# A four-byte GpSimd copy ahead of GpSimd's last five additions, in an attention and mixture-of-experts kernel

## The chip, the cores and the metric

The kernel runs on one core of a Trainium2 chip. The metric is the device time of one execution in microseconds (us); lower is better. Times given are medians of several runs. The engines are TensorE (matrix products, PE in the profile; its weight loads are PEld), VectorE (DVE), ScalarE (ACT), GpSimd (POOL) and SyncE (SP), which here only issues transfers. Each engine runs its own instructions in order and waits on semaphores for the others.

## What is computed

The reference is linear attention with an exponential feature map, and then a layer of eight experts whose outputs are mixed by a normalised routing table `P`:

```python
proj = x @ w_phi; proj -= max(abs(proj))
phi(x) = concat(exp(proj), exp(-proj))
num = phi(q) @ (phi(k).T @ v);  den = phi(q) @ phi(k).sum() + 1e-6
x = num / den                          # 4608 x 512
...
for e in range(8):
    h = maximum(x @ w1[e], 0)          # 512 -> 1024
    out += P[:, e:e+1] * (h @ w2[e])   # 1024 -> 512
```

The change concerns the last two additions into `out`, for expert 7 and the last rows.

## The kernel before

The 4608 rows are nine groups of 512. Attention comes first, together with expert 0; then experts 1 to 7 each go over the groups. For every group the products with `w1` and `w2` are done by a Strassen scheme of seven products on quarters, with sums and differences of quarters made beforehand.

`down7(e, g, H, B7, last)` makes the second product of group `g` and expert `e`. Its left operands are the quarters of the hidden layer `H` and four sums of them, `S[0]` to `S[3]`, made by VectorE as eight instructions of 128x512 (line 1013, in the helper `sub`): each of the four in two halves `h`. `S[3]`, half 1, is the last of the eight. For the very last call, group 7 of expert 7 (`last`), these four stand in buffers of the ring `hT`, so the profile calls them hT; for other groups they are called S.

The seven products, eight matmuls each, are called X1, Y1, Z1, X2, X3, Z2, X4. They go into three PSUM banks: X1, X2, X3 and X4 accumulate in one bank, Z1 and Z2 in another. After each product its bank is read out, scaled by the column of `P`, and added to a quarter of the accumulator `acc[g]`; the next product into the same bank has to wait for that read. There are two ways to read. VectorE does it in one instruction per 128x256 (line 1306). Or ScalarE copies the scaled bank into a buffer `U` or `V` (line 1316, two instructions) and GpSimd adds the 128x512 buffer to `acc` (line 1320).

The last two groups of expert 7 are 6 and 7; they are called a and b here. Their fourteen products are asked for in the order `END` (line 1390). In group 6 only aX1 goes by way of GpSimd; in group 7 bX1, bY1, bZ1 and bX3 do. These are GpSimd's last five additions. aX1 and aY1 add to the same quarter of `acc[6]`, so VectorE's accumulation for aY1 waits for GpSimd's addition for aX1. Stores of finished quarters (line 982) are issued by SP; nine of them belong to these two groups.

What sets the order of instructions is the class `Plan`. Each operation is recorded with the engine it runs on, an estimated duration, and keys that it reads and writes. `schedule` lays the operations out in time by these, and the program is then written in that order. Keys are only names for the planner: the semaphore waits of the program come from the memory that instructions read and write. `"sums of h"` is such a key. It is written by the last difference of each group, and the five last additions read it (line 1323). So the planner places them behind the last difference of group 7, but nothing in the memory that they touch makes them wait for it on the chip.

Of the kernel before, what the change touches and what calls it, by code (L numbers as in the profile page):

```python
# [9 lines left out]
FP32 = mybir.dt.float32  # L10
# [218 lines left out]
def kernel(  # L229
# [11 lines left out]
    nc = tc.nc  # L241

    B, H, S, D = q.shape
# [57 lines left out]
    def pool(el, fn, r=(), w=()):  # L301
        plan.op("POOL", el * 1.64e-3 + 0.17, 0.25, fn, r, w, shared=True)
# [56 lines left out]
    def new(tag):  # L359
        return banks.new(int(tag[1])) if tag in ("P1", "P2") else R[tag].new()  # L360
# [472 lines left out]
    for i, (queue, eng) in enumerate((("ACT", nc.scalar), ("POOL", nc.gpsimd))):  # L833
        dma(queue, 1 << 15, 100, lambda i=i, eng=eng: eng.dma_start(
            out=wphi_f[64 * i:64 * i + 64, :], in_=w_phi), w=[f"wphi_f{i}"])
# [4 lines left out]
    for i in range(2):  # L840
        dve(64, lambda i=i: nc.vector.tensor_copy(
            out=wphi2[64 * i:64 * i + 64, i, :], in_=wphi_f[64 * i:64 * i + 64, :]),
# [4 lines left out]
    for h0 in (4, 6):  # L847
# [3 lines left out]
        out=wgate, in_=moe_w_gate.rearrange("(c p) e -> p c e", p=128)), w=["wgate"])  # L851
# [157 lines left out]
    def sub(eng, el, out_, x, y, op, r, w):  # L1009
        f = nc.vector if eng is dve else nc.gpsimd  # L1010
        kw = {"shared": True} if eng is dve else {}
        eng(el * 0.6 if eng is dve else el * 1.04 + 128,
            lambda: f.tensor_tensor(out=out_(), in0=x(), in1=y(), op=op), r, w, **kw)  # L1013
# [228 lines left out]
    def down7(e, g, H, B7, last=False):  # L1242


        def part(i, j, h):
            return lambda: H[j][h]()[:, :, 256 * i:256 * i + 256]

        def hk(i, j, h=None):
            if h is None:
                return hk(i, j, 0) + hk(i, j, 1)  # L1250
            return [(H[j][h], i)] if g == 8 else [(H[j][h], n) for n in range(2)]
# [5 lines left out]
        S = [new("hT" if last else "S") for _ in range(4)]  # L1257

        def sv(n):
            return S[n]().rearrange("p a b -> p (a b)").rearrange("p (a b) -> p a b", a=4)  # L1260

        def sh(n, h):
            return lambda: sv(n)[:, 2 * h:2 * h + 2, :]
# [22 lines left out]
        for h in range(2):  # L1286
            sub(dve, 512, sh(3, h), part(0, 1, h), sh(1, h), ALU.subtract,
                [(S[1], h)] + hk(0, 1, h), [(S[3], h)] + (["sums of h"] if h else []))

        def prod(bank, lhs, y, r, first, more=()):  # L1290
            f, r2 = B7[y]
            product(bank, lhs, lambda k: f()[:, k, :], 4,
                    r + r2 + (["P"] if e else late) + list(more), first)
# [32 lines left out]
        if e == 1 and g < 9:  # L1326
            for ts in range(4):
                act(512, lambda ts=ts: nc.scalar.activation(
                    out=acc[g][:, ts, :], in_=acc[g][:, ts, :], func=ACT.Copy, bias=0.0,
# [64 lines left out]
    def pop():  # L1394
        if not queue:
            return None
        e, g, H, B7 = queue.pop(0)
        return down7(e, g, H, B7, (e, g) == (E - 1, 7))

    for e in range(1, E):  # L1400
        w1, w2 = load_w(e, ["late"] + [("acc", 8, ts, j) for ts in range(4) for j in range(2)
                                       if e > 1])
        if e == 1:
# [3 lines left out]
            for p in range(4):  # L1407
                seen = {}
# [52 lines left out]
```

## Time and profile before

| | |
|---|---|
| median of 3 runs | 1035.03 us (1034.81 to 1035.73) |
| the profiled execution, its own time | 1034.76 us |
| its span in the profile | 1032.9 us |
| TensorE busy | 1007.7 us (98% of the span) |
| VectorE busy | 874.4 us (85%) |
| ScalarE busy | 707.5 us (68%) |
| GpSimd busy | 466.8 us (45%) |
| mean granted TensorE clock | 0.997 |

The profile comes from one execution. All times in it count from the start of its span. A matmul's end is modelled, and successive matmuls overlap in the record, so their pace is read from one start to the next. The timeline merges instructions of one kind that follow each other: start, length from the first start to the last end, what, and how many. Brackets hold the idle time before, and who ended it. The granted clock is the share of its full speed that TensorE's clock had.

### The profile page before, as it was taken

The page shows a single profiled execution, that of the slowest core. Times are in us where ns is not written, and L with a number is a line of the kernel's source. Part 1 is how long each engine was busy: PE and PEld are TensorE (multiplying, and loading weights), DVE is VectorE, ACT ScalarE, POOL GpSimd, SP SyncE. Part 2 cuts the span into 40 slices and gives each one's busy share as a digit, 9 for nine tenths or more (in the row PEclk, how much of TensorE's full clock was granted, in tenths as well). Part 3 has the DMA queues.
Part 4 walks back from the last instruction along what each step waited for, and adds up shares of the span by engine and source line. Part 5 has one row for each costly group of instructions (what it writes and reads, how often), then busy time and mean ns, then how long its engine had stood idle before and what let it go on. Part 6 is the DMA issues. An engine that isn't in the chain of part 4 may idle for free.

```text
span 1032.9 us, 21788 instructions
## 1 busy us (share of the span) xinstructions
PE 1007.7 (98%) x7856; PEld 692.4 (67%) x7974; DVE 874.4 (85%) x1875; ACT 707.5 (68%) x1571; POOL 466.8 (45%) x535
## 2 busy tenths in 40 slices
PE   7899999999999999999999999999999999999997
PEld 5666666644566766676667666676667666776665
DVE  7999998987787888888878888888888888887887
ACT  7999999845688766566666665666666665656662
POOL 5877775400244444434444354435343444344443
PEclk9999999999999999999999999999999999999998
DMA  9998985095311152122511161106111421104323
GB/s 259 179 171 143 183 156 103 2 230 145 75 43 51 52 107 58 42 63 51 114 42 54 40 128 48 41 22 123 48 47 52 99 65 42 62 22 123 133 92 123
DMA packets 124700, 93.77 MB, mean 91 GB/s; under 512 B 47456, under 2 KB 116640, under 8 KB 124592
## 3 DMA queue, kind: packets, MB, share of 16 engines
q1 hardware_dynamic: 90832, 68.44, 24.3%
q0 software_dynamic: 33680, 23.90, 16.2%
q8 instruction: 62, 1.02, 0.4%
q14 instruction: 46, 0.38, 0.1%
q10 hardware_dynamic: 80, 0.03, 0.0%
HBM read 94.98 MB, written 14.16 MB: 106 GB/s over the span
## 4 chain that ended last, share of the span: by engine, by line
PE 90%; DVE 6%; DMA 1%; issue 1%; ACT 1%; SPq 0%; POOL 0%; DVEq 0%; ACTq 0%
PE P L1130 40%; PE P L1164 30%; PE P L484 17%; DVE acc L1306 1%; PE P L683 1%; DMA acc<-in_q_dram 1%; DVE hT L1194 1%; DVE m L476 1%; DVE w L1013 1%; PE P L722 1%; DVE hT L1013 1%; DVE S L1013 0%; SPq L406 0%; PE P L688 0%; DVE xb L703 0%
## 5 line engine op out<-in xcount | busy, mean ns | idle before, releaser
L1320 POOL TENSOR_TENSOR acc<-acc,V 128x512 f32<-128x512 f32 x244 | 313.9, 1298 | 433.4 <-ACT V L1316 430.0
L1190 ACT COPY U<-P 128x512 f32<-128x512 f32 x378 | 216.2, 588 | 133.4 <-PE P L1164 68.9
L1316 ACT ACTIVATE V<-P 128x256 f32<-128x256 f32 x488 | 212.8, 477 | 122.1 <-PE P L1130 118.6
L1194 DVE CUSTOM_DVE_ANT_0 hT<-P,U 128x512 bf16<-128x512 f32 x378 | 252.3, 687 | 36.6 <-ACT U L1190 21.0
L1130 PEld LDWEIGHTS <-S 128*128 128x128 bf16 x1984 | 194.5, 98 | 56.0 <-issue 3.0
L1306 DVE SCALAR_TENSOR_TENSOR acc<-P,acc 128x256 f32<-128x256 f32 x384 | 164.7, 478 | 72.4 <-PE P L1130 69.9
L1164 PE MATMUL P<-xT,w 128*128 128x512 bf16 x682 | 193.3, 379 | 1.8 <-DVE acc L1306 0.6
L1130 PEld LDWEIGHTS <-hT 128*128 128x128 bf16 x1544 | 151.4, 98 | 56.4 <-DVE hT L1194 0.7
L1164 PE MATMUL P<-xT,T 128*128 128x512 bf16 x544 | 156.8, 379 | 1.6
L1130 PE MATMUL P<-w,hT 128*128 128x256 bf16 x1016 | 146.7, 273 | 0.4 <-DVE hT L1194 0.3
L1130 PE MATMUL P<-T,S 128*128 128x256 bf16 x1056 | 137.7, 273 | 2.8 <-DVE acc L1306 2.6
L1164 PEld LDWEIGHTS <-w 128*128 128x128 bf16 x896 | 87.6, 98 | 61.2 <-issue 0.7
L1130 PE MATMUL P<-w,S 128*128 128x256 bf16 x928 | 124.1, 273 | 1.1
L1013 DVE TENSOR_TENSOR S<-hT 128x512 bf16<-128x512 bf16 x248 | 105.1, 439 | 19.3 <-PE P L1130 18.3
L1164 PEld LDWEIGHTS <-T 128*128 128x128 bf16 x672 | 65.7, 98 | 58.0 <-issue 1.8
L476 DVE TENSOR_REDUCE m<-P 128x4 f32<-128x512 f32 x128 | 83.7, 679 | 3.4 <-PE P L484 2.4
L609 POOL TENSOR_TENSOR v<-v_m,em 128x512 bf16<-128x512 f32 x64 | 66.9, 1045 | 43.2 <-ACT em L480 39.1
L1199 ACT ACTIVATE hT<-P 128x512 bf16<-128x512 f32 x126 | 74.2, 598 | 11.7 <-PE P L1164 11.4
L484 PE MATMUL P<-xT,w 128*128 128x512 bf16 x271 | 71.7, 379 | 0.9 <-ACT q L480 0.3
L1130 PE MATMUL P<-T,hT 128*128 128x256 bf16 x528 | 71.3, 275 | 0.0
L484 PE MATMUL P<-w,hT 128*128 128x512 bf16 x272 | 69.7, 379 | 0.8 <-DVE m L476 0.2
L480 ACT ACTIVATE k<-P 128x512 bf16<-128x512 f32 x128 | 68.8, 633 | 2.2 <-PE P L484 1.3
(109 smaller groups left out, 1178.5 us busy)
## 6 DMA issues: line engine op xcount, KB each, us to landing
xT<-xd SPq DMA_DIRECT2D x168, 128.0 KB, 2.2
w<-in_moe_w_dram POOLq DMA_DIRECT2D x14, 1024.0 KB, 9.9
v_m<-in_v_dram SPq DMA_DIRECT2D x14, 512.0 KB, 5.1
out_dram<-acc SPq DMA_DIRECT2D x12, 512.0 KB, 3.1
X<-xd SPq DMA_DIRECT2D x42, 128.0 KB, 2.2
early<-xd SPq DMA_DIRECT2D x42, 128.0 KB, 2.2
xd<-S SPq DMA_DIRECT2D x18, 256.0 KB, 2.9
qk<-in_k_dram POOLq DMA_DIRECT2D x12, 256.0 KB, 5.5
```

Of the source, the lines that this page charges most:

```text
L476: dve(el, lambda: nc.vector.tensor_reduce(out=dst(), in_=src(), axis=AX.X, op=ALU.max, apply_absolute_value=True), r, w)
L480: act(el, lambda: nc.scalar.activation(out=dst(), in_=src(), func=ACT.Exp, bias=0.0, scale=scale), r, w)
L484: nc.tensor.matmul(out_, lhsT=lhsT, rhs=rhs, start=start, stop=stop)
L1013: lambda: f.tensor_tensor(out=out_(), in0=x(), in1=y(), op=op), r, w, **kw)
L1130: pe(256, lambda i=i, k=k, z=z: nc.tensor.matmul(bank()[:, 256 * i:256 * i + 256], lhsT=lhs(k, i), rhs=rhs(k), start=first and z, stop=k = ...
L1164: pe(512, lambda k=k: nc.tensor.matmul(bank[fp](), lhsT=f()[:, k, 128 * fp:128 * fp + 128], rhs=rhs(k), start=first and k == 0, stop=k == ...
L1190: act(512, lambda: nc.scalar.copy(out=u[fp][n]().rearrange("p a b -> p (a b)"), in_=x[fp]()), [x[fp]], [u[fp][n]])
L1194: dve(500, lambda: nc.vector._custom_dve(ADD_SAT, out=out_(fp, i, j), in0=halves_(bank[fp]()), in1=flat(u[fp][n]()), s0=3.0e38, s1=0.0), [ ...
L1199: act(512, lambda: nc.scalar.activation(out=out_(fp, i, j), in_=halves_(x[fp]()), func=ACT.Relu, bias=0.0, scale=1.0), [x[fp]], [okey(fp, ...
L1306: dve(330, lambda n=n, ts=ts: nc.vector.scalar_tensor_tensor(out=acc[g][:, ts, 256 * j:256 * j + 256], in0=bank()[:, 256 * n:256 * n + 256 ...
L1316: act(390, lambda n=n: nc.scalar.activation(out=u()[:, n, :], in_=bank()[:, 256 * n:256 * n + 256], func=ACT.Copy, bias=0.0, scale=P[:, 4 ...
L1320: pool(670, lambda: nc.gpsimd.tensor_tensor(out=acc[g][:, 2 * i:2 * i + 2, 256 * j:256 * j + 256], in0=acc[g][:, 2 * i:2 * i + 2, 256 * j: ...
```

## The change

When `down7` is called for group 7 of expert 7, one GpSimd copy is recorded behind the differences. It copies one 32-bit word per partition, the last two bf16 columns of `S[3]`, half 1, into a fresh buffer that nothing reads. For the planner it also writes `"sums of h"`.

```diff
         for h in range(2):
             sub(dve, 512, sh(3, h), part(0, 1, h), sh(1, h), ALU.subtract,
                 [(S[1], h)] + hk(0, 1, h), [(S[3], h)] + (["sums of h"] if h else []))
+        if last:
+            seen = new("rr")
+            pool(4, lambda: nc.gpsimd.tensor_copy(
+                out=seen()[:, 0:1], in_=sv(3)[:, 3, 254:256].bitcast(FP32)),
+                [(S[3], 1)], [seen, "sums of h"])
```

The order of TensorE, VectorE and ScalarE stays as it was. On two engines something moves. First GpSimd's end, from the last addition of group 5 on. Rows show the line, the operation, what it writes and reads, its size, and the semaphores that it waits for, which are named after the engine that raises them. acc6_4271 and acc7_4272 are the accumulators of groups 6 and 7. Before:

```order
L1320 TENSOR_TENSOR acc5_4270<-acc5_4270,V_13995 128x2x256 [waits Activation_49]
L1320 TENSOR_TENSOR acc6_4271<-acc6_4271,U_14057 128x2x256 [waits Activation_49]
L1320 TENSOR_TENSOR acc7_4272<-acc7_4272,U_14068 128x2x256 [waits Activation_49]
L1320 TENSOR_TENSOR acc7_4272<-acc7_4272,U_14097 128x2x256 [waits Activation_49,Pool_49]
L1320 TENSOR_TENSOR acc7_4272<-acc7_4272,U_14112 128x2x256 [waits Activation_49]
L1320 TENSOR_TENSOR acc7_4272<-acc7_4272,U_14162 128x2x256 [waits Activation_49,Pool_49]
```

These are the additions for aX1, bY1, bX1, bZ1 and bX3. The same place in the changed program, where line 1320 has become line 1325, and L1291 is the copy:

```order
L1325 TENSOR_TENSOR acc5_4270<-acc5_4270,V_13995 128x2x256 [waits Activation_49]
L1291 COPY rr_14090<-hT_14077 128x1 [waits DVE_49]
L1325 TENSOR_TENSOR acc6_4271<-acc6_4271,U_14057 128x2x256 [waits Activation_49]
L1325 TENSOR_TENSOR acc7_4272<-acc7_4272,U_14068 128x2x256 [waits Activation_49]
L1325 TENSOR_TENSOR acc7_4272<-acc7_4272,U_14114 128x2x256 [waits Activation_49]
L1325 TENSOR_TENSOR acc7_4272<-acc7_4272,U_14099 128x2x256 [waits Pool_49]
L1325 TENSOR_TENSOR acc7_4272<-acc7_4272,U_14163 128x2x256 [waits Activation_49,Pool_49]
```

The copy, with its wait for VectorE, stands ahead of all five additions, and the additions for bZ1 and bX1 have changed places (third and fourth). Second, SP's stores of the two groups; the first six of the nine, before:

```order
L982 DMA out_0_dram<-acc6_4271 128x2x256 [waits DMAHW3_49,DVE_49,Pool_49]
L982 DMA out_0_dram<-acc7_4272 128x2x256 [waits DMAHW4_49,Pool_49]
L982 DMA out_0_dram<-acc6_4271 128x2x256 [waits DMAHW5_49,DVE_49]
L982 DMA out_0_dram<-acc6_4271 128x2x256 [waits DMAHW6_49,DVE_49]
L982 DMA out_0_dram<-acc7_4272 128x2x256 [waits DMAHW7_49,DVE_49]
L982 DMA out_0_dram<-acc6_4271 128x256 [waits DMAHW0_49,DVE_49]
```

and in the changed program:

```order
L982 DMA out_0_dram<-acc6_4271 128x2x256 [waits DMAHW3_49,DVE_49,Pool_49]
L982 DMA out_0_dram<-acc6_4271 128x2x256 [waits DMAHW4_49,DVE_49]
L982 DMA out_0_dram<-acc7_4272 128x2x256 [waits DMAHW5_49,Pool_49]
L982 DMA out_0_dram<-acc6_4271 128x2x256 [waits DMAHW6_49,DVE_49]
L982 DMA out_0_dram<-acc7_4272 128x2x256 [waits DMAHW7_49,DVE_49]
L982 DMA out_0_dram<-acc6_4271 128x256 [waits DMAHW0_49,DVE_49]
```

The store of group 7's first quarter, which waits for GpSimd, has gone from second to third place.

## The prediction

> **What bounds it.** I read the page first, then the chain of waits, then the last 24 us engine by engine. TensorE is busy for 98% of the span and heads the chain nearly throughout, so a change to GpSimd's last five additions can matter only where TensorE stops. The page and the chain (start, length, what) say where:
>
> ```profile
> span 1032.9 us, 21788 instructions
> PEclk9999999999999999999999999999999999999998
> ...
> 1013.25 5.89 DVE hT L1013 x8
> 1019.98 6.21 PE P L1130 x40
> ```
>
> The chain leaves TensorE at 1010 us for VectorE; its largest piece there is the eight differences of the last group (L1013, into hT buffers). The granted clock is full in all slices but the last. TensorE's timeline for the end (start, length from first start to last end, tile, count; in brackets the idle time and its releaser):
>
> ```profile
> 1016.37 1.04 PE L1130 MATMUL P<-T,hT 128*128 128x256 bf16 x8
> 1019.98 1.10 PE L1130 MATMUL P<-T,S 128*128 128x256 bf16 x6 [2.57 <-DVE acc L1306]
> 1020.87 1.92 PE L1130 MATMUL P<-T,hT 128*128 128x256 bf16 x8
> 1022.57 0.63 PE L1130 MATMUL P<-T,S 128*128 128x256 bf16 x2
> 1023.00 1.42 PE L1130 MATMUL P<-w,S 128*128 128x256 bf16 x8
> 1024.26 0.49 PE L1130 MATMUL P<-w,hT 128*128 128x256 bf16 x3
> 1024.59 1.04 PE L1130 MATMUL P<-T,hT 128*128 128x256 bf16 x8
> 1025.46 0.71 PE L1130 MATMUL P<-w,hT 128*128 128x256 bf16 x5
> 1026.01 1.91 PE L1130 MATMUL P<-T,hT 128*128 128x256 bf16 x16
> ```
>
> With a and b for groups 6 and 7, the rows are bZ1, aX3 (six), bX2, aX3 (two), aZ2, bZ2 (three), bX3, bZ2 (five), aX4 with bX4. At full clock eight matmuls take 0.87 us (1024.59 to 1025.46), 0.109 each. bZ1 would hand over at 1016.37 + 0.87 = 1017.24; aX3 starts at 1019.98, 2.74 us late, because VectorE had not yet read aX2 out of the bank that aX3 accumulates into. VectorE's and GpSimd's timelines say why:
>
> ```profile
> 1013.16 5.98 DVE L1013 TENSOR_TENSOR hT<-hT 128x512 bf16<-128x512 bf16 x8
> 1014.50 0.42 DVE L1013 TENSOR_TENSOR hT<-hT 128x512 bf16<-128x512 bf16 x1
> 1014.84 1.49 DVE L1013 TENSOR_TENSOR hT<-hT 128x512 bf16<-128x512 bf16 x1
> 1016.25 1.48 DVE L1013 TENSOR_TENSOR hT<-hT 128x512 bf16<-128x512 bf16 x1
> 1017.66 1.48 DVE L1013 TENSOR_TENSOR hT<-hT 128x512 bf16<-128x512 bf16 x1
> 1019.06 2.43 DVE L1306 SCALAR_TENSOR_TENSOR acc<-P,acc 128x256 f32<-128x256 f32 x6
> 1019.46 0.47 DVE L1306 SCALAR_TENSOR_TENSOR acc<-P,acc 128x256 f32<-128x256 f32 x1
> 1022.82 2.52 DVE L1306 SCALAR_TENSOR_TENSOR acc<-P,acc 128x256 f32<-128x256 f32 x6 [1.33 <-PE P L1130]
> 1026.21 2.62 DVE L1306 SCALAR_TENSOR_TENSOR acc<-P,acc 128x256 f32<-128x256 f32 x6 [0.87 <-PE P L1130]
> 1028.36 0.48 DVE L1306 SCALAR_TENSOR_TENSOR acc<-P,acc 128x256 f32<-128x256 f32 x1
> ...
> 1009.91 1.27 POOL L1320 TENSOR_TENSOR acc<-acc,V 128x512 f32<-128x512 f32 x1 [2.08 <-ACT V L1316]
> 1014.65 1.39 POOL L1320 TENSOR_TENSOR acc<-acc,U 128x512 f32<-128x512 f32 x1 [3.47 <-ACT U L1316]
> 1016.00 1.45 POOL L1320 TENSOR_TENSOR acc<-acc,U 128x512 f32<-128x512 f32 x1
> 1017.55 1.30 POOL L1320 TENSOR_TENSOR acc<-acc,U 128x512 f32<-128x512 f32 x1
> 1018.82 1.44 POOL L1320 TENSOR_TENSOR acc<-acc,U 128x512 f32<-128x512 f32 x1
> ```
>
> The first five differences take 0.42 us each and start 0.335 apart (four steps from 1013.16 to 1014.50). The sixth starts after GpSimd's addition of 1014.65 and takes 1.49; from there a difference ends just after an addition ends (1016.33 after 1016.04, and so on): the two engines take turns. VectorE's accumulations (L1306) take 0.47 beside the addition of 1018.82, so those two don't take turns.
>
> **What the change does.** It removes nothing. It adds one GpSimd copy of four bytes per partition that waits for the eighth difference; behind it on GpSimd's queue stand only the five last additions.
>
> *The differences.* With no addition among them, differences six to eight start at 1014.84, 1015.18 and 1015.51; the last ends at 1015.93 instead of 1019.14, 3.21 us earlier. GpSimd's previous addition, 1009.91 + 1.27, is over before they begin.
>
> *TensorE's stall.* The two accumulations of aX2 follow: the second ended at 1019.46 + 0.47 = 1019.93, and will end at 1016.72. TensorE resumed 0.05 behind it; now it could at 1016.77, while bZ1 keeps it busy to 1017.24. The stall of 2.74 us is gone, with 0.47 to spare.
>
> *The slow stretch behind it.* The rows from 1019.98 on hold 56 matmuls, 55 steps from the first start to the last, which is at 1026.01 + 1.91 - 0.27 = 1027.65 (0.27 is one matmul's length: 1.04 less seven steps). At 0.109 they would take 6.00; they take 7.67, 1.67 more. The rows of 1 us (length, busy time of TensorE, its weight loads, VectorE, ScalarE, GpSimd, then granted clock, DMA share, GB/s) show where:
>
> ```profile
> 1019.00:1020.00 1.00, 0.02 (x1) 0.02 (x1) 1.00 (x4) 0.00 (x0) 1.00 (x1) 1.00 0.00 0
> 1020.00:1021.00 1.00, 1.00 (x7) 0.80 (x7) 1.00 (x3) 0.00 (x0) 0.26 (x1) 0.68 0.00 0
> 1023.00:1024.00 1.00, 1.00 (x7) 0.77 (x6) 1.00 (x3) 0.00 (x0) 0.00 (x0) 0.61 0.96 344
> 1024.00:1025.00 1.00, 1.00 (x11) 0.90 (x10) 1.00 (x4) 0.00 (x0) 0.00 (x0) 1.00 0.03 8
> 1030.00:1031.00 1.00, 0.00 (x0) 0.00 (x0) 0.00 (x0) 0.00 (x0) 0.00 (x0) 0.80 0.95 344
> 1031.00:1032.00 1.00, 0.00 (x0) 0.00 (x0) 0.00 (x0) 0.00 (x0) 0.00 (x0) 0.50 0.10 34
> ```
>
> The clock halves at about 1020.36 (0.68 = 1 - 0.64/2) and is whole again at 1023.78; it halves once more near 1030.6, after TensorE has finished. The slow stretch lasts 3.42 us, and in as long a stretch before each halving TensorE had been idle for most of the time (2.57 before the first, 2.7 before the second: it ends at 1027.92). I take the stall as the cause and count the 1.67 as gained. [...]
>
> So the last matmul starts 2.74 + 1.67 = 4.41 us earlier, at 1023.24, if nothing else stops TensorE. By the same steps it reaches aX3 at 1017.24, bX2 at 1017.89, aZ2 at 1018.98, bX3 at 1020.18, aX4 at 1021.6. bX3 waits for VectorE's read of bX2: last bX2 matmul ends about 1018.92, two accumulations 0.39 apart end at 1019.83. bX2 and bZ2 wait for ScalarE's reads of bX1 and bZ1, over at 1016.57 + 1.71 = 1018.28:
>
> ```profile
> 1016.57 1.71 ACT L1316 ACTIVATE U<-P 128x256 f32<-128x256 f32 x4 [1.26 <-PE P L1130]
> 1025.72 0.84 ACT L1316 ACTIVATE U<-P 128x256 f32<-128x256 f32 x2 [7.44 <-PE P L1130]
> 1026.70 1.26 POOL L1320 TENSOR_TENSOR acc<-acc,U 128x512 f32<-128x512 f32 x1 [6.44 <-ACT U L1316]
> L641 POOL COPY r<-r_r x32: 174/184/227, 14.9 to 197.1; 128x2 f32<-128x2 f32 x32
> 1027.11 0.37 SPq L982 DMA_DIRECT2D out_dram<-acc  x1
> 1029.28 0.49 SPq L982 DMA_DIRECT2D out_dram<-acc  x1
> ```
>
> *The copy and the additions behind it.* No such copy from VectorE's result stands in the trace. The nearest row, GpSimd's copies of 128x2, has a median of 184 ns (minimum, median, maximum in the row); the start after a release is bounded by 0.14 (ScalarE done at 1026.56, GpSimd at 1026.70). I take 0.32 for both, with 0.17 as the low end and one whole addition, 1.3, as the high end. The first addition then starts at 1016.25, 1.6 us later than before, and ends at 1017.5. Only aY1's accumulation on VectorE waits for it, due at 1017.43: nothing. It would hold bX2's read, and so TensorE, if it ended 0.9 us later still.
>
> *The stores.* SP issues in order, and its third store of these two groups (acc7, upper left quarter) now waits for the fourth addition, bX1's, since bZ1's goes first. At 1.27 to 1.39 per addition (alone; as in the four rows above) the fourth ends between 1021.3 and 1021.7. That store and the six behind it are five of 256 KB and two of 128 KB, 1.57 MB, 4.57 us at 344 GB/s. Before, the last five (1.05 MB, 3.05 us) moved from 1028.05, 0.94 after the issue of 1027.11, to 1031.1. Now seven in a row move from 1022.3 to 1022.7 until 1026.9 to 1027.3, against 1031.1 - 4.41 = 1026.7. The tail gives back 0.2 to 0.6; I take 0.4. VectorE's last accumulation ends at 1028.84 - 4.41 = 1024.43, GpSimd's last addition near 1023.5; neither ends later than the stores.
>
> *Sum.* 2.74 + 1.67 - 0.4 = 4.0 us. The profiled execution itself took 1034.76 (1.86 around its span), 0.27 under the median: 1035.03 - 4.0 = 1031.0 us. With all ends, 3.1 (copy at 1.3: the stores move with it one for one) to 4.4: 1030.6 to 1031.9.
>
> **Rivals.** *The clock halves anyway*, for a cause other than the stall: the 1.67 stays, the gain is 2.3, 1032.7. For it: the gap lasted 2.57 us only. Against: no other slice of the page shows a lowered clock, and both drops follow an idle TensorE. 8%. [...]
>
> *The collision moves to the accumulations.* The additions now lie at 1016.25 to 1021.7, beside some twelve accumulations of L1306. If those took turns with them as the differences did, each of the four additions would hold one up by 1.06 (1.48 - 0.42) and two more at their ends, 5 to 6 us on VectorE, which TensorE's reads wait for: 1035.0 - 4.0 + 5.5 = 1036.5, slower. It decides from 4 us of such waits. For it: the accumulations also read SBUF. Against: the 0.47 beside the addition of 1018.82. 5%.
>
> *The copy doesn't hold the additions back* (released early, or the eighth difference isn't what decides): 1035.0. Against: GpSimd's order has the copy first, waiting for VectorE. 4%.
>
> *The copy or its release is dear, or a late store order costs more*: a gain of 2 to 3, 1032.5. 4%.
>
> **How the numbers follow.** The forecast holds with 79%: 1031.0. A measurement of this kernel can tell about 0.2%, 2.07 us, from no change: under 1032.96 counts as faster. Faster: 79, and most of the clock's and the dear copy's cases (6 and 3): 0.88. Same: the idle copy and the rest of those two: 0.07. Slower: 0.05. The range takes the forecast's own bounds with 0.5 us of spread between runs below, and the clock case above: 1030.1 to 1032.8.
>
> **What would show it.** Right: eight differences of 0.42 in some 2.8 us instead of 5.98; a GpSimd copy near 1016; no idle time of TensorE over 0.2 us behind bZ1; clock 1.00 to TensorE's end; matmuls ending near 1023.5; additions of 1.27 to 1.4 after the copy. Wrong: a difference over 1 us, an accumulation over 0.6, a halved clock before the last matmul, TensorE waiting for aY1's or bX2's read, or stores still moving three us after the last accumulation.

## The result and the profile after

The changed kernel takes 1030.94 us (median of 7 runs, 1030.73 to 1032.11), the kernel before in the same session 1034.84 (7 runs, 1033.29 to 1035.73). The ratio is 0.9966, with a 95% interval of 0.9954 to 0.9977: 3.9 us faster. The forecast was 1031.0, between 1030.1 and 1032.8. The profiled execution of the changed kernel itself took 1030.93 us.

The page after, with the span and the granted clock in 40 slices:

```profile
span 1029.1 us, 21788 instructions
PEclk9999999999999999999999999999999999999999
```

The last slice, 8 before, is 9 now. The end of the chain of waits after (start, length, what):

```profile
1014.88 7.16 PE P L1130 x64
...
1022.07 2.23 DVE acc L1311 x5
```

Before, the chain spent 5.89 us on the eight differences and came back to TensorE at 1019.98. Now TensorE runs through from 1014.88, and no difference is in the chain of the end. (Lines behind the change stand five higher: L1311 are VectorE's accumulations, L1325 GpSimd's additions, L1321 ScalarE's reads.) VectorE's and GpSimd's timelines after, with the last two differences, the first two accumulations (those of aX2) and the last one, and all of GpSimd's end:

```profile
1015.43 0.41 DVE L1013 TENSOR_TENSOR hT<-hT 128x512 bf16<-128x512 bf16 x1
1015.76 0.42 DVE L1013 TENSOR_TENSOR hT<-hT 128x512 bf16<-128x512 bf16 x1
1016.10 0.47 DVE L1311 SCALAR_TENSOR_TENSOR acc<-P,acc 128x256 f32<-128x256 f32 x1
1016.49 0.47 DVE L1311 SCALAR_TENSOR_TENSOR acc<-P,acc 128x256 f32<-128x256 f32 x1
...
1020.41 0.48 DVE L1311 SCALAR_TENSOR_TENSOR acc<-P,acc 128x256 f32<-128x256 f32 x1
...
1024.21 0.47 DVE L1311 SCALAR_TENSOR_TENSOR acc<-P,acc 128x256 f32<-128x256 f32 x1
...
1016.24 0.19 POOL L1291 COPY rr<-hT 128x1 f32<-128x1 f32 x1 [4.80 <-DVE hT L1013]
1016.38 1.27 POOL L1325 TENSOR_TENSOR acc<-acc,U 128x512 f32<-128x512 f32 x1
1017.61 1.27 POOL L1325 TENSOR_TENSOR acc<-acc,U 128x512 f32<-128x512 f32 x1
1018.83 1.28 POOL L1325 TENSOR_TENSOR acc<-acc,U 128x512 f32<-128x512 f32 x1
1020.06 1.28 POOL L1325 TENSOR_TENSOR acc<-acc,U 128x512 f32<-128x512 f32 x1
```

The copy waits in front of the additions until the eighth difference is over (1016.18). No difference lasts longer than 0.42, and the accumulations beside the additions last 0.47 to 0.48 throughout. TensorE's timeline after, from bZ1 on, the first two rows and the last, and its clock:

```profile
1016.62 1.04 PE L1130 MATMUL P<-T,hT 128*128 128x256 bf16 x8
1017.50 0.82 PE L1130 MATMUL P<-T,S 128*128 128x256 bf16 x6
...
1021.86 1.91 PE L1130 MATMUL P<-T,hT 128*128 128x256 bf16 x16
...
1021.00:1022.00 1.00, 1.00 (x12) 0.90 (x10) 0.67 (x2) 0.42 (x2) 0.34 (x1) 1.00 0.16 56
...
1026.00:1027.00 1.00, 0.00 (x0) 0.00 (x0) 0.00 (x0) 0.00 (x0) 0.00 (x0) 0.64 0.95 343
1027.00:1028.00 1.00, 0.00 (x0) 0.00 (x0) 0.00 (x0) 0.00 (x0) 0.00 (x0) 0.50 0.22 77
```

aX3 follows bZ1 after 0.88 us, with no idle time. The clock (the figure behind POOL's share, seventh in a row) is whole until TensorE has been done for 2.5 us. From bZ1's start to the start of the last matmul (1021.86 + 1.91 - 0.27 = 1023.50) it takes 6.88 us; before it was 1027.65 - 1016.37 = 11.28. That is 4.40 us gained. Two things take from it. The transfers of the stores run on to 1027.22, 2.54 us behind the end of VectorE's last accumulation (1024.68); before that was 1031.1 - 1028.84 = 2.26, so 0.28 is given back. And this execution came to bZ1 0.25 us later than the one before (1016.62 against 1016.37), which no part of the change explains. 4.40 - 0.28 - 0.25 = 3.87; the spans differ by 3.8. The second and third of the nine stores after, as SP issues them:

```profile
1020.91 0.38 SPq L982 DMA_DIRECT2D out_dram<-acc  x1
1021.39 0.42 SPq L982 DMA_DIRECT2D out_dram<-acc  x1
```

### The profile page after: what moved, and what is told of

Read it like the earlier page. It is cut to its first block, busy times and chain, and to the rows that moved or that the text cites. A ratio compares the mean times of both kernels' runs of the same rounds, so it can differ in the third digit from the quotient of the medians.

```text
span 1029.1 us, 21788 instructions
## 1 busy us (share of the span) xinstructions
PE 1005.7 (98%) x7856; PEld 691.3 (67%) x7974; DVE 870.9 (85%) x1875; ACT 706.8 (69%) x1571; POOL 466.4 (45%) x536
## 4 chain that ended last, share of the span: by engine, by line
PE 91%; DVE 5%; issue 1%; SPq 1%; DMA 1%; ACT 1%; POOL 0%; DVEq 0%; ACTq 0%
PE P L1130 40%; PE P L1164 31%; PE P L484 17%; PE P L683 1%; DVE acc L1311 1%; DVE hT L1194 1%; DMA acc<-in_q_dram 1%; DVE m L476 1%; DVE w L1013 1%; PE P L722 1%; SPq L406 0%; PE P L688 0%; DVE xb L703 0%; ACT q L480 0%; SPq L462 0%
## 5 line engine op out<-in xcount | busy, mean ns | idle before, releaser
L1325 POOL TENSOR_TENSOR acc<-acc,V 128x512 f32<-128x512 f32 x244 | 313.9, 1298 | 433.4 <-ACT V L1321 430.0
L1321 ACT ACTIVATE V<-P 128x256 f32<-128x256 f32 x488 | 212.3, 476 | 122.3 <-PE P L1130 119.1
L1311 DVE SCALAR_TENSOR_TENSOR acc<-P,acc 128x256 f32<-128x256 f32 x384 | 164.6, 477 | 71.3 <-PE P L1130 68.8
```

Source lines behind the costliest of these rows:

```text
L1311: dve(330, lambda n=n, ts=ts: nc.vector.scalar_tensor_tensor(out=acc[g][:, ts, 256 * j:256 * j + 256], in0=bank()[:, 256 * n:256 * n + 256 ...
L1321: act(390, lambda n=n: nc.scalar.activation(out=u()[:, n, :], in_=bank()[:, 256 * n:256 * n + 256], func=ACT.Copy, bias=0.0, scale=P[:, 4 ...
L1325: pool(670, lambda: nc.gpsimd.tensor_tensor(out=acc[g][:, 2 * i:2 * i + 2, 256 * j:256 * j + 256], in0=acc[g][:, 2 * i:2 * i + 2, 256 * j: ...
```

## The experiments

All were timed in three rounds beside the kernel before, whose medians were 1034.72, 1035.0 and 1034.82 us in the three sessions. In all of them TensorE, VectorE and ScalarE keep their order, apart from what an edit adds.

### Is it the wait, or the new order of two additions?

The change did two things: the additions wait, and bZ1's goes ahead of bX1's. First the new order almost without the wait: the copy reads the first difference.

```diff
-                out=seen()[:, 0:1], in_=sv(3)[:, 3, 254:256].bitcast(FP32)),
+                out=seen()[:, 0:1], in_=sv(0)[:, 0, 0:2].bitcast(FP32)),
```

> The copy reads the first of the eight differences instead of the last; the program's order stays that of the changed kernel. Theory (GpSimd's additions and VectorE's differences take turns, and the copy gains by keeping them apart): the additions start as early as before the change, the last three differences take about 1.48 us each again, TensorE idles about 2.6 us behind bZ1, and the time is that of the kernel before, 1034.8 us (1034 to 1035.5). Rival (the gain comes from the new order of the third and fourth addition and of the stores, or from the copy's mere presence): differences of 0.42 us or no idle time of TensorE, and 1031 us.

1032.61 us (1031.87 to 1033.76), ratio 0.998, interval 0.997 to 0.9989: between the two. GpSimd's, VectorE's and TensorE's timelines of this kernel:

```profile
1013.78 0.32 POOL L1291 COPY rr<-hT 128x1 f32<-128x1 f32 x1 [2.46 <-DVE hT L1013]
1014.79 1.39 POOL L1325 TENSOR_TENSOR acc<-acc,U 128x512 f32<-128x512 f32 x1 [0.70 <-ACT U L1321]
1016.14 1.45 POOL L1325 TENSOR_TENSOR acc<-acc,U 128x512 f32<-128x512 f32 x1
1018.50 1.27 POOL L1325 TENSOR_TENSOR acc<-acc,U 128x512 f32<-128x512 f32 x1 [0.92 <-ACT U L1321]
...
1014.97 1.49 DVE L1013 TENSOR_TENSOR hT<-hT 128x512 bf16<-128x512 bf16 x1
1016.38 1.48 DVE L1013 TENSOR_TENSOR hT<-hT 128x512 bf16<-128x512 bf16 x1
1017.79 0.41 DVE L1013 TENSOR_TENSOR hT<-hT 128x512 bf16<-128x512 bf16 x1
...
1019.04 0.82 PE L1130 MATMUL P<-T,S 128*128 128x256 bf16 x6 [1.50 <-DVE acc L1311]
```

The third addition is now bZ1's and has to wait for ScalarE (0.92), since bZ1 is read later than bX1. The eighth difference finds GpSimd idle and is free; only the sixth and seventh collide. TensorE is idle for 1.50 instead of 2.57, and its clock stays whole. So the new order alone brings some 2 us of the 3.9, by taking one collision and the halved clock away. The theory had forecast none of the gain here and the rival all of it; neither had seen that it would split.

Then the wait without the new order: the kernel before, with the copy written inside the first of the five additions, so that every order is the old one.

```diff
+            def add():
+                if ending and tail:
+                    nc.gpsimd.tensor_copy(out=xT[:, 2, 0:2].bitcast(FP32),
+                                          in_=tail.pop()().bitcast(FP32))
-            pool(670, lambda: nc.gpsimd.tensor_tensor(
+                nc.gpsimd.tensor_tensor(
...
+            pool(670, add,
```

Here `tail` holds the last two columns of `S[3]`, half 1, of the last call.

> The kernel before with the same one-word copy of the last difference ahead of GpSimd's five additions, but written inside the first of them, so that all orders stay as before: bX1's addition ahead of bZ1's, and the stores in the old order. Theory (the wait does it all, the new order of two additions is worth nothing behind the wait): all eight differences 0.42 us, no idle time of TensorE behind bZ1, clock whole, about 1030.9 us. Rival (part of the gain is the new order, worth some 2.1 us as in the run with the copy of the first difference): differences or accumulations still collide somewhere, 1032 to 1033 us.

1030.48 us (1029.96 to 1030.80), ratio 0.9956, interval 0.994 to 0.9973. The last difference, the last accumulation, the copy with the first addition, the second store, TensorE at bZ1, aX3 and the end, and the last transfers:

```profile
1015.09 0.42 DVE L1013 TENSOR_TENSOR hT<-hT 128x512 bf16<-128x512 bf16 x1
...
1023.54 0.48 DVE L1310 SCALAR_TENSOR_TENSOR acc<-P,acc 128x256 f32<-128x256 f32 x1
...
1015.64 0.19 POOL L1326 COPY xT<-hT 128x1 f32<-128x1 f32 x1 [4.88 <-DVE hT L1013]
1015.78 1.27 POOL L1328 TENSOR_TENSOR acc<-acc,U 128x512 f32<-128x512 f32 x1
...
1019.65 0.38 SPq L982 DMA_DIRECT2D out_dram<-acc  x1
...
1015.95 1.04 PE L1130 MATMUL P<-T,hT 128*128 128x256 bf16 x8
1016.82 0.82 PE L1130 MATMUL P<-T,S 128*128 128x256 bf16 x6
...
1021.19 1.91 PE L1130 MATMUL P<-T,hT 128*128 128x256 bf16 x16
...
1026.00:1027.00 1.00, 0.00 (x0) 0.00 (x0) 0.00 (x0) 0.00 (x0) 0.00 (x0) 0.50 0.27 98
```

From bZ1 to the last matmul it takes 6.88 us here too (1021.19 + 1.64 - 1015.95). So the wait alone brings the whole gain, and behind it the new order of two additions is worth nothing to TensorE. It costs something at the stores: the last accumulation ends at 1024.02 and the transfers at 1026.27, 2.25 later, as before the change and not 2.54 as after it. In the old order the second store waits for GpSimd's third addition (over at 1019.63 here) and is issued at 1019.65; in the new order the second one waits for the accumulation of aX3. The 0.28 given back is thus the price of the new order. The other traces agree: with the old order the transfers end 2.23 to 2.28 us behind the last accumulation in all five (the kernel before, this one, the filler matmuls, and GpSimd's fills and copies below). With the new order it is about 2.5 in seven of eight; with 16 fills on VectorE, where the last matmuls came so late that the earlier stores had gaps between them, it is 2.24. The median is 0.46 under the changed kernel's, but they ran in different sessions and the intervals overlap, so only the trace shows this kernel ahead.

### What the halved clock was worth, and what causes it

In the kernel before, twelve matmuls of 128x512 that compute nothing needed are put behind bZ1, where TensorE idled.

```diff
             prod(z, s(0), "t1", sk(0), True, sk(3))
+            if last:
+                f = new("P1")
+                for _ in range(12):
+                    plan.op("PE", 0.0, 0.0, lambda: nc.tensor.matmul(
+                        f(), lhsT=xT[:, 2, 0:128], rhs=xT[:, 2, 0:512],
+                        start=True, stop=True, skip_group_check=True), [z], [f])
```

> The kernel before, with twelve 512-column matmuls (0.216 us each, 2.6 us together, their result unused) on TensorE behind bZ1, where it stood idle. Nothing else moves; the stall stays as long as it was. Theory (the idle time is what halves the clock for 3.4 us): the granted clock stays 1.00 to the end, the 55 steps to the last matmul take 6.0 us instead of 7.67, and the time is 1034.8 - 1.67 = 1033.2 us. Rival (the clock halves there for another cause): the clock falls to 0.5 after 1020 as before and the time stays 1034.8 us.

1033.3 us (1032.86 to 1034.72), ratio 0.999, interval 0.9981 to 1.0. TensorE's timeline and the clock where it was halved before:

```profile
1016.41 1.04 PE L1130 MATMUL P<-T,hT 128*128 128x256 bf16 x8
1017.29 2.75 PE L1348 MATMUL P<-xT 128*128 128x512 bf16 x12
1020.03 0.81 PE L1130 MATMUL P<-T,S 128*128 128x256 bf16 x6
...
1021.00:1022.00 1.00, 1.00 (x12) 0.89 (x10) 0.79 (x3) 0.00 (x0) 0.00 (x0) 1.00 0.00 0
```

The three slow differences and the late aX3 are as before (1020.03 - 1016.41 = 3.62, against 3.61), but the clock is whole (1.00 from 1021 to 1022, where the kernel before had 0.50). So in this kernel TensorE's 2.57 us of idle time are what halved the clock, and filling them gains 1.4 us by the medians (the interval just reaches no change), for 1.67 in the trace. The remaining 2.4 us, down to the changed kernel, are the stall itself (2.74) less the stores (0.28).

The granted clock that is on record for each single execution, as a mean over its span, says the same for more than one trace. Of the 57 executions of the kernel before in the three sessions, 30 had 0.997 or less, with a median of 1035.1 us, and 19 had 0.999 or more, with a median of 1033.4. All ten executions with the filler matmuls had 0.998 or more, and their median, 1033.3, is that of the kernel before when its clock was 0.999 or more. So the stall probably halved the clock in a part of the executions only, and the change is worth 3.9 us over the median execution and some 2.4 over those 19. A mean over the span doesn't say where the clock was low, so this is not shown for each execution by itself.

Then the stall is put back into the changed kernel by another way: VectorE fills a scratch area 16 times, or 8 times, between the last difference and its read of aX2, with no collision.

```diff
+        def do():
+            f.tensor_tensor(out=out_(), in0=x(), in1=y(), op=op)
+            for n in range(late):
+                nc.vector.memset(xT[:, 2 + n % 2, n // 2 * 512:][:, 0:512], 0.0)
```

`late` is 16 or 8 for the eighth difference of the last call and 0 elsewhere. First what was expected of 16 fills, then of 8.

> [...] Theory: TensorE idles 3.1 - 0.47 = 2.6 us behind bZ1 although no difference is slow, the clock halves behind it, and the time is about that of the kernel before, 1030.9 + 2.6 + 1.7 - 0.3 = 1034.9 us. Rival (the clock halves for another cause than TensorE's idle time): 1030.9 + 2.6 - 0.3 = 1033.2 us. Rival (the early differences are not what the gain hangs on): 1031 us.

> [...] Theory: TensorE idles 1.55 - 0.47 = 1.1 us, and so short a pause leaves the clock whole: 1032.0 us. If any pause halves the clock: 1033.6 us.

With 16 fills 1036.33 us (1034.02 to 1037.52), ratio 1.0013, interval 1.0001 to 1.0025; with 8 fills 1033.35 (1031.85 to 1033.8), ratio 0.9981, interval 0.9964 to 0.9998. A fill took 0.27 us, so 4.4 and 2.2 us in all. TensorE's timelines and clock, first with 16:

```profile
1021.46 1.44 PE L1134 MATMUL P<-T,S 128*128 128x256 bf16 x6 [3.62 <-DVE acc L1316]
...
1020.00:1021.00 1.00, 0.00 (x0) 0.00 (x0) 0.99 (x5) 0.00 (x0) 1.00 (x2) 0.54 0.00 0
1026.00:1027.00 1.00, 1.00 (x7) 0.69 (x6) 0.53 (x2) 0.00 (x0) 0.00 (x0) 0.54 0.00 0
```

and with 8:

```profile
1019.90 0.81 PE L1134 MATMUL P<-T,S 128*128 128x256 bf16 x6 [1.43 <-DVE acc L1316]
...
1020.00:1021.00 1.00, 1.00 (x11) 0.89 (x10) 1.00 (x4) 0.00 (x0) 1.00 (x2) 1.00 0.00 0
```

The late read of aX2 stopped TensorE for 3.62 us with 16 fills and for 1.43 with 8, without any collision of differences. Behind the idle time of 1.43 the clock stayed whole. Behind the one of 3.62 it was halved from 1020.08 to 1026.92: 6.84 us, twice the 3.42 that the kernel before showed behind 2.57 us of idleness.

Both runs were slower than forecast (1034.9 and 1032.0). No run shows the 3.1 and 1.55 us that the two sums take for the fills, against the 4.4 and 2.2 measured; a fill of the same size at line 828 of the kernel before, 0.272 in its trace, had the price. With 16 fills the longer slow stretch comes on top. With 8 fills the median is near the 1033.6 of the other theory, that any pause halves the clock. The trace speaks against that theory: the clock is whole, and from bZ1 to the last matmul it takes 8.47 us, 1.59 more than in the changed kernel, which would give some 1032.5. Of the rest, the traced execution (1033.78) shows 0.81 as a later start of bZ1 (1017.43), after a clock of 0.91 in its first 20 us; for the other executions the cause is open.

### What collides

In the kernel before the five additions are left out, and in place of each GpSimd fills its 128x512 buffer `u` three times (it writes and reads nothing), or copies it onto itself twice (it reads one operand and writes).

```diff
+                if ending:
+                    for _ in range(3):
+                        nc.gpsimd.memset(u(), 0.0)
+                    return
```

```diff
+                if ending:
+                    for _ in range(2):
+                        nc.gpsimd.tensor_copy(out=u(), in_=u())
+                    return
```

> The kernel before, with each of GpSimd's last five additions left out and three fills of its 128x512 input buffer in its place, which read nothing from memory and are released by the same read of ScalarE. The output lacks those five additions. Theory (the two engines take turns only where GpSimd reads): the eight differences take 0.42 us each though GpSimd is busy beside them, no stall, about 1030.9 us. Rival (any GpSimd work holds the differences up): three or more differences over 0.8 us, and 1032 us or more.

> The kernel before, with each of GpSimd's last five additions left out and two copies of its 128x512 input buffer onto itself in its place: one input instead of two. The output lacks those five additions. Theory (a GpSimd instruction that reads takes turns with the differences, whatever the number of its inputs): the differences that meet a copy each last until the copy ends; with copies shorter than the 1.27 us of an addition the last difference is late by less than 3.2 us, and the time lies between 1031.5 and 1035 us. Rival (it takes two inputs on GpSimd): differences of 0.42 us and about 1030.9 us.

Fills: 1030.59 us (1030.37 to 1031.38), ratio 0.9962, interval 0.9949 to 0.9976. Copies: 1031.52 (1031.17 to 1033.19), ratio 0.9972, interval 0.996 to 0.9984. VectorE's and GpSimd's timelines with fills, the seventh difference and the second fill:

```profile
1016.18 0.42 DVE L1013 TENSOR_TENSOR hT<-hT 128x512 bf16<-128x512 bf16 x1
...
1016.23 0.52 POOL L1323 MEMSET U<- 128x512 f32 x1
```

and with copies, the seventh difference and the second copy (the sixth and the eighth difference took 0.83 and 0.82):

```profile
1016.17 0.83 DVE L1013 TENSOR_TENSOR hT<-hT 128x512 bf16<-128x512 bf16 x1
...
1016.03 0.69 POOL L1323 COPY U<-U 128x512 f32<-128x512 f32 x1
```

A difference, which has two operands in SBUF, took 0.42 us beside GpSimd's fills, which only write, 0.83 beside its copies, which read one operand, and 1.49 beside its additions, which read two. So these differences were held up by the instructions of GpSimd that read, and one operand was enough. The accumulations, which have one operand in PSUM, took 0.47 to 0.48 beside the additions; no run varied their operands, so what spares them was not shown.

### When must GpSimd be released?

The copy was released by earlier differences than the eighth, to see how many collisions come back. The edit is the one shown for the first difference, with another source: `sv(1)[:, 3, 254:256]` for the fourth, `sv(2)[:, 0, 0:2]` for the fifth, `sv(2)[:, 3, 254:256]` for the sixth. A last one copies all 128x512 of the sixth:

```diff
-                out=seen()[:, 0:1], in_=sv(3)[:, 3, 254:256].bitcast(FP32)),
+                out=xT[:, 2, 0:512].rearrange("p (a b) -> p a b", a=2), in_=sh(2, 1)()),
```

> The copy reads the fifth difference: two differences are left to meet an addition. Theory: the seventh and eighth take about 1.45 us, the last ends about 2.1 us later than in the changed kernel, TensorE idles 2.1 - 0.47 = 1.6 us, and the time is 1030.9 + 1.6 = 1032.5 us if so short a pause leaves the clock whole, up to 1.7 more if it halves. Rival (each collision costs the same everywhere, no slack): 1033.0 us without the clock. Rival (only a wait for the last difference counts): 1034.8 us.

> The copy reads the sixth difference: one difference is left to meet an addition. Theory: only the eighth takes about 1.45 us, it ends 1.06 us later than in the changed kernel, TensorE idles 1.06 - 0.47 = 0.6 us, clock whole, 1031.5 us. Rival (no slack on TensorE): 1032.0 us. Rival (only a wait for the last difference counts): 1034.8 us.

> The changed kernel with the copy reading a word of the fourth difference instead of the eighth. Released during the fifth difference, as the first addition before was. Theory (what decides is how short the copy is: a short one finds no gap between differences that are already queued): the copy lasts until the eighth difference is over, near 1016.3, differences all 0.42 us, about 1031.0 us. Rival (what decides is where in the row of differences it is released: up to the fifth it gets its turn, as the copy of the first difference did in 0.32 us): the copy is over by 1015.2, the additions follow at once and differences six to eight take 1.4 to 1.5 us each where an addition lies beside them, 1032.6 us or more.

> The changed kernel with the copy reading all 128x512 of the sixth difference (output into a scratch area that nothing reads later), instead of one word of the eighth. Theory (a short copy is held, a long one gets its turn): the copy starts near 1015.4, lasts 0.7 to 0.8 us, the seventh or eighth difference takes 0.8 us or more, and the additions behind it may collide with the eighth; 1031.2 to 1032 us. Rival (what decides is the place in the row: from the fifth difference on nothing of GpSimd gets in): the copy is shown as long as 1 us or more, until the eighth difference is over, all differences 0.42 us, about 1031.2 us with the additions 0.4 us later than behind the one-word copy.

| copy released by | copy lasts | slow differences | median us | ratio, interval |
|---|---|---|---|---|
| first | 0.32 | 6th, 7th | 1032.61 | 0.998, 0.997 to 0.9989 |
| fourth | 0.32 | 7th, 8th | 1032.64 | 0.998, 0.9971 to 0.9989 |
| fifth | 0.99 | none | 1031.05 | 0.9966, 0.9952 to 0.998 |
| sixth | 0.65 | none | 1030.81 | 0.9964, 0.9951 to 0.9977 |
| sixth, 128x512 | 1.01 | none | 1031.02 | 0.9966, 0.9953 to 0.9979 |
| eighth (the change) | 0.19 | none | 1030.94 | 0.9966, 0.9954 to 0.9977 |

The timelines of GpSimd and VectorE with the copy of the fifth difference and with the 128x512 copy of the sixth, each with the last difference of its kernel:

```profile
1015.78 0.99 POOL L1291 COPY rr<-hT 128x1 f32<-128x1 f32 x1 [3.80 <-DVE hT L1013]
...
1016.30 0.42 DVE L1013 TENSOR_TENSOR hT<-hT 128x512 bf16<-128x512 bf16 x1
```

```profile
1015.22 1.01 POOL L1291 COPY xT<-hT 128x512 bf16<-128x512 bf16 x1 [4.20 <-DVE hT L1013]
...
1015.35 0.42 DVE L1013 TENSOR_TENSOR hT<-hT 128x512 bf16<-128x512 bf16 x1
```

The theories for the fifth and the sixth, that fewer collisions would come back one by one, failed: none came back. A copy that became ready during the sixth or seventh difference lasted until the eighth was over (1016.77 against 1016.72 with the fifth; the 128x512 copy until 1016.23, 0.46 behind the eighth's 1015.77). One that became ready during the second or fifth was through in 0.32, and the additions behind it then took turns with two of the last differences (1.49 and 1.48 us with the copy of the first). The size didn't decide: the 128x512 copy was held like the one-word copy (1.01 us, against 0.99 with the fifth), and slowed no difference. What decides who goes next is open. The place in the row fits all five copies, but additions that were queued did win against the seventh and the eighth difference in the kernel before (1.48 us each), so the place alone is no rule.

## Why the prediction was right

- **The differences.** Forecast: the eighth ends 0.44 us ahead of bZ1's start (1015.93, 1016.37). Measured: 1016.18 against 1016.62, 0.44.
- **TensorE's stall.** Forecast 2.74 removed, with 0.47 to spare. The second accumulation of aX2 ended at 1016.96, so aX3 could have started at 1017.01 and did at 1017.50: 0.49 to spare. The late reads confirm the path from the other side.
- **The slow stretch.** Forecast 1.67. bZ1 to the last matmul shortened by 4.40 us, for 2.74 + 1.67 = 4.41. That the idle time causes it was taken on weak ground (two drops of the clock, each behind an idle TensorE). The filler matmuls show it, and with them the first rival fell. That the 1.67 counts in full was luck in part: of the 57 executions of the kernel before, 19 had a clock of 0.999 or more and were 1.8 us faster at the median than the 30 with 0.997 or less; had most executions been like these, the gain would have been some 2.4.
- **The copy.** Forecast 0.32 from the eighth difference to the first addition, measured 0.20 (1016.18 to 1016.38). The copy held the additions. aY1's accumulation started at 1017.69, behind the end of the first addition (1017.65), and so at most 0.03 late; TensorE didn't feel it.
- **The stores.** The one step that went wrong. Forecast 0.4 given back, because the third store waits for the fourth addition. Measured 0.28, and the store that governs is the second: aX3's accumulation ends at 1020.89, the store is issued at 1020.91, and the eight stores from there (six of 256 KB, two of 128 KB, 1.84 MB, 5.3 us at 344 GB/s) move from about 1021.85 to 1027.2. The third store, behind the fourth addition (over at 1021.34), was issued at 1021.39 and could move from 1022.33, while the second's 256 KB moved until about 1022.6. I had fixed the run of stores at the last one that waits for GpSimd, and not asked from where on the transfers run without a gap.
- **The collision moves to the accumulations.** Fell: they last 0.47 to 0.48 beside every addition. (Its price was summed wrongly: six waits of 1.06 are 6.4 us, not 5 to 6.)

The sum was 4.0, the traces give 4.13 without the 0.25 that this execution came late to bZ1, and the medians 3.9. Its low end, 3.1, doesn't come out of its own terms: 4.41 less 0.6 for the stores and 0.98 for a dear copy is 2.8. The range was wide enough for that. The terms were right; that the time was met within 0.1 us is luck, with single runs of the kernel before over 5 us apart.

What stays open is which executions of the kernel before had the slow stretch. Its single runs lie between 1032.4 and 1038.0 (with one at 1040.96), those of the changed kernel between 1030.7 and 1032.1. The clocks on record fit a clock that is halved in some executions and not in others, but no short run of the kernel before has a trace, and the longest runs are not explained by one such stretch.

## What to carry to other kernels

Where two engines take turns, as VectorE's differences and GpSimd's additions did here (1.48 us for a difference instead of 0.42), look for the instructions that nobody waits for soon. Four 1.3 us additions with slack behind them cost TensorE 2.7 us only because the first became ready in the middle of eight short differences; one copy that waits for the last of these orders the two rows for 0.2 us. Count an idle time of TensorE as a stall, and ask for the slow clock behind it too: here 2.57 us of idleness cost another 1.67 in the trace, and 1.43 or 1.50 us cost nothing more. For the end of a kernel whose last work is stores, find the point from which the transfers run without a gap; here the store that opens this stretch, issued at 1020.91, set the end at 1027.22, and the planner's small exchange of two stores cost 0.28 us.

## What the hardware showed unexpectedly

The clock. Over all thirteen traces the halving came between 2.2 and 4.9 us after TensorE's last matmul had ended: 2.24 with 16 fills, 2.51 after the change (1023.77 to 1026.28, from the 0.64 in the row of 1026 after it), 4.92 at the end of the run with the copy of the sixth difference (1023.68 to 1028.60), and 3.64 at the end of the run with filler matmuls (1026.30 to 1029.94):

```profile
1024.39 1.91 PE L1130 MATMUL P<-T,hT 128*128 128x256 bf16 x16
...
1029.00:1030.00 1.00, 0.00 (x0) 0.00 (x0) 0.00 (x0) 0.00 (x0) 0.00 (x0) 0.97 0.47 167
```

Where TensorE had work again, the slow stretch lasted 3.42 us (kernel before) or 6.84 (16 fills). What sets the delay and the length was not shown, nor why the idle time would halve the clock in some executions only, as the clocks on record suggest.

The turns. A GpSimd copy of four bytes that was ready waited 0.99 us while two more differences went by, though the queued additions of the kernel before got every second turn (three differences of 1.48 to 1.49). So this short copy, beside a row of VectorE's, held GpSimd back for longer than its own wait says.
